# Engine programs in the main body instead of a block with a closing all-engine barrier

## The chip, the core and the metric

The kernel runs on one core of a Trainium2 chip. A core has five engines with an instruction stream each: TensorE (PE), VectorE (DVE), ScalarE (ACT), GpSimd (POOL) and SyncE (SP), which here issues 97 of the 98 transfers in the trace of before. In this kernel they meet only through semaphores (counters that one engine raises and another waits for). The time is in device microseconds (us), one number for each execution. Every execution also has a **span**: from the first to the last instruction that the profile records. Time and span are not the same, and this study is about the difference; I call it the **rest** (time less span of the same execution). Spans are listed to 0.1 us, so a single rest is good to about 0.05 us, plus the scatter between runs.

## The reference

One layer on 2048 tokens of width 640, in bfloat16: a layer norm, then a linear attention with 32 heads and a gated MLP side by side, and a residual.

```
xn  = layernorm(x)
out = x + linear_attention(xn; wqkv, w_phi, wo) + (silu(xn @ w1) * (xn @ w3)) @ w2
```

Its mathematics plays no part in what follows.

## The kernel before

The kernel records all operations in a list and orders them with a greedy scheduler of its own. It then makes one list per engine from them, of waits and operations with their semaphore updates. At the end of SyncE's list stand waits for all 17 output stores:

```python
    def emit(self, finish):
        ...
        for o in self.ops:
            ...                      # waits that o still needs, then o and what it signals
        for o in finish:             # the 17 output stores
            lists["SP"].append(("wait", o.sem[2], o.sem[1]))
        return lists
```

The lists are played into the five bodies of a block. Leaving the block emits an all-engine barrier:

```python
    lists = P.emit(finish)

    def play(items, eng):
        for it in items:
            if it[0] == "wait":
                eng.wait_ge(it[1], it[2])
            else:
                r = it[1]()
                if it[2] is not None:
                    r.then_inc(it[2], it[3])

    with nc.allow_low_precision(...), nc.allow_non_contiguous_dma(...), nc.Block() as block:

        @block.sync
        def _(e):
            play(lists["SP"], nc.sync)

        @block.tensor
        def _(e):
            play(lists["PE"], nc.tensor)
        ...                          # scalar, vector, gpsimd alike
```

A second all-engine barrier, at the entry, comes with the creation of the program object and stays (GpSimd's gathering starts at 0.600 us and the last engine is released by 0.783 us).

The softmax here doesn't subtract the row's maximum and nothing guards it: scores larger than these inputs give would overflow.

## Time and profile before

| | before |
|---|---|
| time, median of the first three runs | 267.78 us (267.52 to 267.91) |
| profiled execution: time, span, rest | 267.64, 265.86, 1.78 us |
| TensorE busy | 262.1 us, 99% of the span |
| last matmul done | 263.56 us |
| issue of the last output store | 263.92 us |
| end of the span | 265.86 us |

The page begins with the span and the busy time of each engine (PEld is TensorE's weight load):

```profile
span 265.9 us, 4695 instructions
...
PE 262.1 (99%) x1891; PEld 155.9 (59%) x1891; DVE 183.9 (69%) x313; ACT 106.3 (40%) x226; POOL 95.9 (36%) x107
...
PE 96%; DVE 1%; DMA 1%; POOL 0%; issue 0%
```

The last of these lines is the page's chain of work that ended last. The same chain in order of time (start, length, what) ends so:

```profile
7.07 0.05 issue
7.11 256.46 PE PS L104 x1867
263.57 0.02 issue
263.60 0.29 DVE xres L104
```

TensorE runs without a gap that the chain would name from 7.11 us to 263.57 us. So nothing in the middle can be won by changing how programs begin and end. The chain stops at VectorE's 0.29 us and doesn't tell of the 2 us behind it. What SyncE waits for from 264 us to the end does (waits in that window: us in total, times, longest):

```profile
SPq L929 <- DMA out_dram<-xres: 0.7, 2, 0.4
SPq L116 <- DVE xres L104: 0.2, 1, 0.2
SPq L935 <- PEq L935: 0.2, 1, 0.2
```

L929 is the waits on the output stores. L935 is the block: the closing barrier, where SyncE waits for its release. (The view names TensorE's sequencer; by the records below it is GpSimd that releases.) The views count semaphores, drains and jumps as no work, so here are the sequencers' records of the tail, taken from the trace (start in us, length in ns):

```
217.648  2669  POOL  drain                    (block)
225.259   629  ACT   drain, signals           (block)
262.251  1355  PE    drain, signals           (block)
263.611   330  DVE   drain, signals           (block)
263.917   332  SP    issue of the last store, 128x128
264.300    28  SP    wait for two stores; six of these follow, to 265.142
265.403    28  SP    wait for the last store and an older one
265.471    41  SP    jump, carrying the wait for one more old store
265.648     7  SP    drain, signals           (block)
265.681    17  POOL  has all four signals
265.759    17  POOL  releases the others
265.801    17  SP    released; ACT 265.805, DVE 265.812, PE 265.813 (51 ns: end of span)
```

### The profile page before, as it was taken

The numbers are of one execution on the slowest core, as the hardware profiler recorded it, in microseconds if no ns is written. First come the engines' busy times: TensorE is split into PE (matmuls) and PEld (weight loads), VectorE is DVE, ScalarE is ACT, GpSimd is POOL, SyncE is SP. The second block draws the span as 40 slices with busy tenths as digits, with TensorE's granted clock in tenths as the row PEclk, the third lists the DMA queues.
The fourth block names the chain that finished last, engine by engine and source line by source line (L and its number), as shares of the span: only waits on it lengthen the run. The fifth ranks groups of instructions, "written<-read, shape, count | busy, mean of one in ns | idle before, by whom it ended". The sixth has DMA issues, their size and how long they took to land.

```text
span 265.9 us, 4695 instructions
## 1 busy us (share of the span) xinstructions
PE 262.1 (99%) x1891; PEld 155.9 (59%) x1891; DVE 183.9 (69%) x313; ACT 106.3 (40%) x226; POOL 95.9 (36%) x107
## 2 busy tenths in 40 slices
PE   7999999999999999999999999999999999999996
PEld 3655545565558556465565756455656564777773
DVE  4668999999796679696685858788769567512112
ACT  5546988699760452251405240263143322000000
POOL 4221587989997035106030523007303321000000
DMA  6997088723301981932525070613260626141211
GB/s 211 270 307 205 8 161 242 162 52 55 117 2 22 270 195 39 140 56 62 94 49 128 2 159 25 131 25 75 62 133 22 132 52 128 27 123 52 87 39 49
DMA packets 62742, 27.73 MB, mean 104 GB/s; under 512 B 49920, under 2 KB 62720, under 8 KB 62720
## 3 DMA queue, kind: packets, MB, share of 16 engines
q1 hardware_dynamic: 62576, 27.26, 44.0%
q8 instruction: 15, 0.25, 0.4%
q10 hardware_dynamic: 144, 0.16, 0.2%
q14 instruction: 7, 0.06, 0.1%
HBM read 12.81 MB, written 2.62 MB: 58 GB/s over the span
## 4 chain that ended last, share of the span: by engine, by line
PE 96%; DVE 1%; DMA 1%; POOL 0%; issue 0%
PE PS L104 96%; DMA x_tok<-in_A_x_dram 1%; DVE bst L104 1%; DVE x_tok L104 0%; DVE mv L104 0%; POOL rstd L104 0%; DVE xres L104 0%
## 5 line engine op out<-in xcount | busy, mean ns | idle before, releaser
L104 PE MATMUL PS<-xnT,w_s 128*128 128x512 bf16 x480 | 108.2, 379 | 0.0
L104 PEld LDWEIGHTS PS<-xnT,w_s 128*128 128x128 bf16 x480 | 46.4, 98 | 50.9
L104 POOL TENSOR_TENSOR eqt<-eqt,rS 128x600 bf16<-128x600 bf16 (+1 forms) x32 | 41.0, 1306 | 97.4 <-DVE rS L104 97.4
L104 ACT ACTIVATE th<-PS 128x512 f32<-128x512 f32 x48 | 28.6, 596 | 79.0 <-PE PS L104 78.9
L104 PE MATMUL PS<-w_s,hT 128*128 128x320 bf16 (+2 forms) x384 | 54.9, 299 | 0.0
L104 DVE SCALAR_TENSOR_TENSOR t<-th,PS 128x512 bf16<-128x512 f32 x48 | 32.4, 675 | 31.4 <-ACT th L104 31.4
L104 PEld LDWEIGHTS PS<-w_s,hT 128*128 128x128 bf16 x384 | 37.1, 98 | 15.1
L104 PE MATMUL PS<-WVK,xnT 128*128 128x512 bf16 (+3 forms) x260 | 45.6, 330 | 0.1
L104 POOL TENSOR_TENSOR ekt<-ekt,rS 128x640 bf16<-128x640 bf16 x32 | 39.8, 1276 | 4.8 <-DVE rS L104 4.8
L104 ACT ACTIVATE eqt<-PS 128x240 bf16<-128x240 f32 (+1 forms) x96 | 27.2, 348 | 25.9 <-PE PS L104 24.1
L104 DVE TENSOR_TENSOR xres<-PS,xres 128x640 bf16<-128x640 f32 (+2 forms) x17 | 13.3, 782 | 33.5 <-PE PS L104 33.5
L104 PEld LDWEIGHTS PS<-WVK,xnT 128*128 128x128 bf16 x260 | 24.2, 98 | 19.4 <-ACT WVK L104 0.4
L104 DVE SCALAR_TENSOR_TENSOR hT<-t,PS 128x512 bf16<-128x512 bf16 x48 | 33.0, 687 | 1.7
L104 DVE TENSOR_REDUCE S<-ekt 128x64 f32<-128x1280 bf16 x16 | 23.3, 1455 | 2.2 <-ACT ekt L104 2.1
L104 PE MATMUL PS<-wo_s,oT 128*128 128x320 bf16 (+2 forms) x160 | 24.5, 299 | 0.0
L104 PE MATMUL PS<-Wqp,xnT 128*128 128x360 bf16 (+1 forms) x160 | 24.3, 299 | 0.0
L104 DVE TENSOR_REDUCE S<-eqt 128x66 f32<-128x1320 bf16 x16 | 24.2, 1510 | 0.0
L104 ACT ACTIVATE ekt<-PS 128x640 bf16<-128x640 f32 x32 | 22.3, 703 | 1.3 <-PE PS L104 0.8
L104 PEld LDWEIGHTS PS<-Wqp,xnT 128*128 128x128 bf16 x160 | 15.2, 98 | 7.6
L104 DVE RECIPROCAL rS<-S 128x64 f32<-128x64 f32 (+1 forms) x32 | 17.9, 560 | 1.1
L104 PEld LDWEIGHTS PS<-wo_s,oT 128*128 128x128 bf16 x160 | 15.2, 98 | 5.9
L104 DVE TENSOR_TENSOR o_tok<-PS,g_s 128x360 bf16<-128x360 f32 (+1 forms) x32 | 15.7, 491 | 1.1
(50 smaller groups left out, 124.3 us busy)
## 6 DMA issues: line engine op xcount, KB each, us to landing
w_s<-in_B_w_dram SPq DMA_DIRECT2D x6, 640.0 KB, 6.4
xres<-in_A_x_dram SPq DMA_DIRECT2D x16, 160.0 KB, 2.5
out_dram<-xres SPq DMA_DIRECT2D x15, 160.0 KB, 1.9
x_tok<-in_A_x_dram SPq DMA_DIRECT2D x3, 640.0 KB, 4.8
w_s<-in_B_w_dram SPq DMA_DIRECT2D x1, 1920.0 KB, 9.3
wo_s<-in_A_wo_dram SPq DMA_DIRECT2D x1, 800.0 KB, 4.8
WVK<-in_A_wqkv_dram SPq DMA_DIRECT2D x2, 320.0 KB, 4.5
x_tok<-in_A_x_dram SPq DMA_DIRECT2D x3, 160.0 KB, 2.7
```

The costliest lines, as they stand in the source:

```text
L104: o = _Op(eng, lambda: m(*args, **kw), r, w, cost)
```

## The change

The intent: no block, so no jumps and no barrier at the end. The waits on the output stores stay on SyncE. The outcome must be the same, since every dependence has its own semaphore.

```diff
-    with nc.allow_low_precision(...), nc.allow_non_contiguous_dma(...), nc.Block() as block:
-
-        @block.sync
-        def _(e):
-            play(lists["SP"], nc.sync)
-        ...                          # tensor, scalar, vector, gpsimd alike
+    with nc.allow_low_precision(...), nc.allow_non_contiguous_dma(...):
+        for e in ("SP", "PE", "ACT", "DVE", "POOL"):
+            play(lists[e], P.eng[e])
```

More of the change, by code (lines that the diff above doesn't have):

```diff
@@ L933, in play @@
                     r.then_inc(it[2], it[3])
-    with nc.allow_low_precision(reason="bf16 results"), nc.allow_non_contiguous_dma(reason="w_phi rows"), nc.Block() as block:
-        @block.sync
-        def _(e):
-            play(lists["SP"], nc.sync)
-        @block.tensor
-        def _(e):
-            play(lists["PE"], nc.tensor)
-        @block.scalar
-        def _(e):
-            play(lists["ACT"], nc.scalar)
-        @block.vector
-        def _(e):
-            play(lists["DVE"], nc.vector)
-        @block.gpsimd
-        def _(e):
-            play(lists["POOL"], nc.gpsimd)
+    with nc.allow_low_precision(reason="bf16 results"), nc.allow_non_contiguous_dma(reason="w_phi rows"):
+        for e in ("SP", "PE", "ACT", "DVE", "POOL"):
+            play(lists[e], P.eng[e])
 _INS = ['A_x', 'A_wqkv', 'A_w_phi', 'A_wo', 'B_x', 'B_w1', 'B_w3', 'B_w2']
```

## The prediction

> What bounds the kernel now. The span is 265.9 us; three timed runs gave a median of 267.78 us. The page shows TensorE busy 262.1 us (99%); the chain in order of time has one unbroken TensorE piece of 256.46 us, from 7.11 to 263.57 us. Before it stand 7 us of loading and normalising; after it 0.29 us of VectorE work, the last output store and the end of the program. The granted clock is 1.000.

> What the change does. The order of instructions shows every engine with the same work in the same order; only the jump at each end of each engine's program is gone. No wait between engines, no tile and no transfer changes. In the built program the jump into a block falls through: no branch record stands there in the trace, and behind the entry barrier, which stays, the first work follows as usual (VectorE after 0.13 us; elsewhere it needs 0.10 us from a semaphore wait to its next work). So the entry can gain 0.00 to 0.03 us.

> What is really removed is the closing barrier. By the sequencers' records in the trace, SyncE's last paired wait for output stores ends at 265.43 us; then come a branch that carries one more wait (265.47 us), SyncE's drain (265.65 us), the gathering on GpSimd's queue (265.68 us), its release (265.76 us) and the receipt on the four others (265.80 to 265.86 us). In the changed program SyncE ends on one more semaphore wait in the branch's place, as long as its others (0.03 us), so at about 265.50 us: 0.36 us off the end of the span. The drains of the four other engines end by 263.94 us and cost nothing now. The waits on the output stores stay, so the 1.5 us from the last store's issue (263.92 us) to the end of its wait stay too.

> All of this 0.36 us is on the critical path. With the entry the span should be about 265.5 us.

> Is it in the time too? The time is 1.9 us longer than the span. [...] I take the whole, plus a few hundredths.

> Prediction: 267.37 us, 0.15% less; 8 times in 10 between 266.9 and 267.8 us, a range made mostly of the spread of single runs (267.52 to 267.91) and of the unknown end of the program. Chances: faster by over 2% 0.01, within 2% 0.98, slower by over 2% 0.01.

> What would show the steps right: the span falls by 0.3 to 0.45 us; no drain stands at the end of any engine; SyncE's last record is a semaphore wait; the unbroken TensorE piece stays at 256.5 us within 0.3 us and begins within 0.1 us of 7.11 us. Wrong: a TensorE piece changed by over 0.5 us[...], or a span shorter by 0.36 us with an unchanged time (then the end outside the span takes the gain back).

> What would make the prediction wrong: the end outside the span costs more or less when engines arrive apart[...].

The sum of the forecast: 0.36 us for the tail, and 0.05 us for the entry (0.00 to 0.03 us) and the "few hundredths" together, make the 0.41 us from 267.78 to 267.37 us.

## More of the kernel before

The length of a drain's record is not a cost: GpSimd's runs from 217.648 to 220.317 us, but GpSimd's last piece of work ends at 220.250 us. The record contains that work.

## The result, and the profile after

| | before | after |
|---|---|---|
| time, median of 6 runs | 267.68 us (267.52 to 268.33) | 266.79 us (266.62 to 267.09) |
| ratio after to before, 95% interval | | 0.9964 [0.9951, 0.9977] |
| profiled execution: time, span, rest | 267.64, 265.86, 1.78 us | 266.92, 265.67, 1.25 us |
| tail: last store's issue to the end of the span | 1.947 us | 1.512 us |
| rest, all fast runs | 1.69 to 1.80 us (25 runs in the jobs below) | 1.19 to 1.26 us (6 runs) |

The ratio is the mean time of one kernel's fast runs over that of the other's of the same rounds, so it is not quite the ratio of the medians quoted here. The change is a gain of 0.4%, clear of noise but small. It is over twice the 0.41 us that I had forecast. It lies below the stated range. All outputs are right.

The page after, for the same lines:

```profile
span 265.7 us, 4684 instructions
...
PE 261.9 (99%) x1891; PEld 155.8 (59%) x1891; DVE 183.9 (69%) x313; ACT 106.2 (40%) x226; POOL 95.9 (36%) x107
...
PE 97%; DMA 1%; DVE 1%; ACT 0%; POOL 0%; issue 0%
```

The chain in order of time after:

```profile
6.66 0.10 issue
6.76 257.06 PE PS L104 x1871
263.81 0.02 issue
263.83 0.29 DVE xres L104
```

Two things mislead here. The span of this one execution fell by only 0.2 us (the six executions of after had spans of 265.4 to 265.9 us), and the TensorE piece looks 0.60 us longer. The piece counts 1871 matmuls in place of 1867: the chain now enters TensorE four matmuls earlier. Measured between the same two matmuls (the 25th and the last to start), TensorE took 256.23 us before and 256.28 us after. Of the 0.24 us by which the last matmul came later, 0.18 us are there at the 25th matmul already (7.30 us in place of 7.11 us). They were collected in the first 7 us, while the first loads land, and they are scatter between executions: three later programs with the same bodies started that matmul at 7.10 or 7.11 us (e5 with TensorE held, e8, e6), others at up to 7.67 us (e9), and e7's disturbed execution at 8.28 us.

Behind the last store the change is plain. SyncE's waits from 264 us on, after; the line of the barrier is gone:

```profile
SPq L929 <- DMA out_dram<-xres: 0.6, 2, 0.4
SPq L116 <- DVE xres L104: 0.2, 1, 0.2
```

And the records of the tail after:

```
264.154   332  SP    issue of the last store
264.538    17  SP    wait for one old store; seven waits for two stores follow
265.638    28  SP    wait for the last store and an older one (end of span)
```

No drain stands at the end of any engine. The records of the entry, up to the first load's issue at 0.805 us and VectorE's first work at 0.883 us, start at the same nanosecond as before, but for one drain of ScalarE that starts 5 ns earlier.

So the time fell by 0.89 us by the medians, or by 0.96 us by the ratio (0.0036 of 267.7 us). The tail gives 1.947 - 1.512 = 0.435 us of it, and the rest gives 1.75 - 1.23 = 0.52 us, in which no record of an instruction lies. Together they make 0.955 us.

### The profile page after: what moved, and what is told of

It reads as the page before. It is cut to its first block, busy times and chain, and to the rows that moved or that the text cites. A ratio compares the mean times of both kernels' runs of the same rounds, so it can differ in the third digit from the quotient of the medians.

```text
span 265.7 us, 4684 instructions
## 1 busy us (share of the span) xinstructions
PE 261.9 (99%) x1891; PEld 155.8 (59%) x1891; DVE 183.9 (69%) x313; ACT 106.2 (40%) x226; POOL 95.9 (36%) x107
## 4 chain that ended last, share of the span: by engine, by line
PE 97%; DMA 1%; DVE 1%; ACT 0%; POOL 0%; issue 0%
PE PS L104 97%; DMA x_tok<-in_A_x_dram 1%; DVE bst L104 0%; ACT xnT L104 0%; POOL rstd L104 0%; DVE x_tok L104 0%; DVE xres L104 0%; DVE mv L104 0%
```

## The experiments

The question that was left open by the views: why do 0.52 us vanish *outside* the span?

- **Theory A**: it is being held back. Behind its last record each engine has an end of the program that no view shows. Without the barrier four engines walk through theirs while SyncE still waits for the stores.
- **Theory B**: the jumps and separate bodies cost it, outside the span, at the entry or the end.
- **Theory C**: the drains cost it; they leave the engines in a state that takes longer to end.

All edits are to the kernel after, unless said. `play` is as above, and `finish[-2:]` are the stores of the last tile's two parts. All figures are of fast runs. The rests are medians of 4 to 6 runs each; those of before, run on the same chip in the same job, had medians of 1.75, 1.73 and 1.74 us in the three jobs. The kernel after itself was not run again in these jobs; its figures are those above.

### e1: the barrier without the block

```diff
         for e in ("SP", "PE", "ACT", "DVE", "POOL"):
             play(lists[e], P.eng[e])
+        nc.all_engine_barrier()
```

> The straight bodies with an all-engine barrier put back behind them: the barrier without the block and its jumps. 'Rest' is a run's time less its own span: 1.78 us in the profiled run of before, 1.22 us after. Theory A (it is the closing barrier: without it the four other engines go ahead into an end of the program that the span doesn't show): all of the gain goes, time as before (267.7 us, ratio 0.999 to 1.001), rest 1.7 to 1.85 us, and the span's tail from the last store's issue to the end again 1.95 us. Theory B (jumps and separate bodies cost the time, at the entry or at the end, outside the span): the rest stays near 1.22 us and only the 0.43 us of the tail come back, time about 267.2 us.

Measured: 267.50 us, ratio to before 0.9995 [0.9972, 1.0018]; rest 1.71 us. Theory B falls: with the straight bodies and no jump, the barrier alone brings the whole rest back. The tail was 1.757 us, not the 1.95 us that I expected. Before's tail thus has two parts: the barrier's (1.757 - 1.512 = 0.245 us) and 0.19 us of the jump that carried a wait.

SyncE's waits from 264 us on, in this kernel (L938 is the barrier):

```profile
SPq L116 <- DVE xres L104: 3.4, 2, 3.2
SPq L929 <- DMA out_dram<-xres: 0.6, 2, 0.4
SPq L938 <- PEq L938: 0.2, 1, 0.2
```

The barrier's line is back with the 0.2 us that it had before. (The 3.4 us of L116 are no change: the issue of the last store but one ends just behind 264 us here, so that its wait of 3.2 us falls into the window.)

### e2: drains, no barrier

```diff
             play(lists[e], P.eng[e])
+        for e in ("SP", "PE", "ACT", "DVE", "POOL"):
+            P.eng[e].drain()
```

> The straight bodies, each closed by a drain of its engine, without any semaphore between engines. Theory A (engines held back to a common end): drains don't hold the early engines, so rest stays about 1.22 us, and the time at most 0.1 us above after (SyncE's own drain). Theory C (the drains themselves cost, GpSimd's above all, in what follows): rest 1.5 to 1.8 us.

Measured: 267.00 us, ratio 0.9971 [0.9947, 0.9995]; rest 1.23 us. Theory C falls. The trace has the same drains as before (GpSimd 2669 ns, TensorE 1355 ns, VectorE 330 ns), only nobody waits for them. (As said, most of each length is the engine's own last work.)

### e3: a barrier without drains

```diff
             play(lists[e], P.eng[e])
+        nc.all_engine_barrier(sem_only=True)
```

> The straight bodies with a barrier made of semaphores alone, no drains. Theory A: rest 1.7 to 1.85 us as with the full barrier, span tail 0.2 to 0.4 us longer than after, time 267.4 to 267.8 us. Theory C (the drains cost): rest about 1.22 us, and only the tail grows.

Measured: 267.51 us by its four fast runs, ratio 0.9994 [0.9969, 1.0018]; rest 1.75 us. Its profiled execution (345.39 us at a granted clock of 0.756, the only one of the 59 executions of changed programs) isn't used for anything. The drains don't matter from this side either.

### e4: all engines wait, without a barrier

```diff
             play(lists[e], P.eng[e])
+        for e in ("PE", "ACT", "DVE", "POOL"):
+            for o in finish[-2:]:
+                P.eng[e].wait_ge(o.sem[2], o.sem[1])
```

> No barrier and no drain: the four other engines themselves wait, as SyncE does, for the landing of the last two output stores, and so end together with SyncE. Theory A: the span stays as after (within 0.1 us in its tail) and the rest rises to 1.7 to 1.85 us, time about 267.3 us: that would show that being held is what costs, not the barrier's own instructions. Theories B and C: rest about 1.22 us and time as after, 266.8 us.

Measured: 267.56 us, ratio 0.9991 [0.9968, 1.0014]; rest 1.76 us, with a tail of 1.542 us. This is the cleanest of the four. There is no gathering, no release, no drain and no jump. In the records all five engines see the last store land between 265.731 and 265.743 us. Yet half a microsecond more passes behind the span. SyncE's waits look as in the kernel after:

```profile
SPq L116 <- DVE xres L104: 3.4, 2, 3.2
SPq L929 <- DMA out_dram<-xres: 0.6, 2, 0.4
```

A reader of these two lines alone would say that nothing had changed (L116 as in e1). Being held is what costs, not the barrier's own instructions.

### e5: one engine held at a time

```diff
             play(lists[e], P.eng[e])
+        for o in finish[-2:]:
+            P.eng["PE"].wait_ge(o.sem[2], o.sem[1])      # or "ACT", "DVE", "POOL"
```

> Only TensorE waits for the last two stores beside SyncE; the other three go ahead. What is asked: is it one engine whose own end outside the span is long (rest 1.75 us for that engine, 1.23 us for the others), or does each held engine add a part (rests between 1.23 and 1.75 us, the sum of the four extras about 0.52 us)? My guess is that the steps behind the kernel pass from engine to engine, so that each held one adds a part: 1.3 to 1.5 us here.

> Only ScalarE waits beside SyncE. One long engine: rest 1.23 or 1.75 us. Parts: 1.3 to 1.5 us.

> Only VectorE waits beside SyncE. One long engine: rest 1.23 or 1.75 us. Parts: 1.3 to 1.5 us.

> Only GpSimd waits beside SyncE. One long engine: rest 1.23 or 1.75 us; were it one engine, GpSimd would be my guess, as its drain is the longest in the trace of before[...]. Parts: 1.3 to 1.5 us.

(GpSimd's drain in the trace of before: a record of 2.67 us, 0.067 us of it behind GpSimd's last work.)

| held beside SyncE | time, median | rest | over SyncE alone |
|---|---|---|---|
| none (after) | 266.79 us | 1.23 us | |
| VectorE | 266.93 us | 1.35 us | 0.12 us |
| ScalarE | 266.91 us | 1.40 us | 0.17 us |
| TensorE | 267.10 us | 1.50 us | 0.27 us |
| GpSimd | 267.42 us | 1.81 us | 0.58 us |

Single rests within a row lie within 0.1 us. Two of the sixteen executions took 269 us (one with TensorE, one with VectorE held); their spans were 2 us longer and their rests the same, so the rest is the sharper measure here. My guess of added parts fails: the four extras sum to 1.14 us, and all engines held together cost 0.53 us. GpSimd alone costs as much as all. That suggests a maximum: each engine has an end of its own length, and the time ends with the last of them. The other pure picture, one long engine and nothing for the rest, fails too, since the three others differ from 1.23 us.

The profile of the kernel with GpSimd held, by its span and its last pieces of work (timeline: start, length, engine, line, what):

```profile
core 0: 265.6 us, clock 1.000
...
263.54 0.88 SPq L116 DMA_DIRECT2D out_dram<-xres  x2
263.77 0.29 DVE L104 TENSOR_TENSOR xres<-PS,xres 128x128 bf16<-128x128 f32 x1 [0.26 <-PE PS L104]
```

And of the kernel after:

```profile
core 0: 265.7 us, clock 1.000
...
263.61 0.88 SPq L116 DMA_DIRECT2D out_dram<-xres  x2
263.83 0.29 DVE L104 TENSOR_TENSOR xres<-PS,xres 128x128 bf16<-128x128 f32 x1 [0.26 <-PE PS L104]
```

By the profile the first of these two executions is the faster one, by 0.05 us. By the measured time it is the slower one, by 0.49 us (267.41 against 266.92 us).

### e7: three held, GpSimd free

```diff
-        for e in ("PE", "ACT", "DVE", "POOL"):
+        for e in ("PE", "ACT", "DVE"):
             for o in finish[-2:]:                          # against e4
                 P.eng[e].wait_ge(o.sem[2], o.sem[1])
```

> TensorE, ScalarE and VectorE wait for the last two stores beside SyncE; GpSimd alone goes ahead. Held alone they gave rests of 1.50, 1.40 and 1.35 us over 1.23 us for SyncE alone. If every engine walks through an end of its own length and the longest sets the time (maximum): 1.50 us. If each held engine adds its part (sum): 1.23 + 0.27 + 0.17 + 0.12 = 1.79 us.

Measured: rest 1.52 us (1.48 to 1.55). The maximum said 1.50 us, the sum 1.79 us: the maximum holds. The times are no use here. Two of four runs were near 269 us, the profiled one (269.22 us) with a clock of 0.994 and its last matmul done at 265.81 us in place of 263.8 us; the rest was the same in all four.

### e8: GpSimd released one store earlier

```diff
             play(lists[e], P.eng[e])
+        o = finish[-2]
+        P.eng["POOL"].wait_ge(o.sem[2], o.sem[1])
```

> GpSimd waits for the last store but one only, which lands 0.29 to 0.30 us before the last; SyncE waits for both. Maximum: GpSimd's end of 1.81 us then starts 0.29 us before the end of the span, so rest 1.51 us (1.45 to 1.58). If it mattered only whether GpSimd waits at all or is the last to come: 1.8 us or 1.23 us.

Measured: rest 1.50 us (1.45 to 1.57), time 266.90 us. In the records GpSimd is released at 265.136 us, 0.288 us before the end of the span at 265.424 us, and 1.81 - 0.29 = 1.52 us. A late GpSimd costs to the extent that it is late, not for waiting as such.

### e6: the final waits on GpSimd alone

```diff
         for o in finish:
-            lists["SP"].append(("wait", o.sem[2], o.sem[1]))
+            lists["POOL"].append(("wait", o.sem[2], o.sem[1]))
```

> All final waits moved from SyncE to GpSimd, so GpSimd alone ends last and SyncE goes ahead. Maximum: rest 1.75 to 1.85 us, as with both held, time 267.3 to 267.5 us, though the program has no barrier and as few instructions as after. If the rest came from two or more engines meeting late: 1.23 us.

Measured: 267.28 us, ratio 0.9980 [0.9958, 1.0003]; rest 1.79 us. SyncE's last record ended at 264.39 us, 1.2 us before the end of the span, and it helped nothing. One engine, the last one and with a long end, is enough. So the kernel after is fast for two reasons at once: nothing holds the others, and the one engine that must wait for the stores is the one with the shortest end.

### e9: the jump without its wait (an edit to the kernel before)

```diff
         @block.sync
         def _(e):
             play(lists["SP"], nc.sync)
+            nc.sync.drain()
```

> The kernel before, with block and barrier, but a drain closes SyncE's body, so that the odd last wait hangs on it and not on the jump: the built program then has no branch that is taken. In the trace of before 0.14 us lie between the branch's end and the drain behind it. Expected: no branch record, tail from the last store's issue 1.95 us down to 1.76 to 1.82 us, rest unchanged at 1.75 us, time 0.13 to 0.19 us below before (the spread of single runs may hide it). If the block itself, not the waits on its jump, costs: tail still 1.95 us.

Measured: no jump is left in the trace; tail 1.823 us in place of 1.947 us; rest 1.73 us. The time (267.60 us, ratio 0.9997 [0.9975, 1.0019]) can't resolve 0.12 us and is inconclusive by itself. By the records, the added drain (266.145 us) takes the wait, and the barrier's drain starts 0.055 us after it; before, 0.177 us passed from the start of the jump to that drain. The block's barrier is unchanged, with the same line in SyncE's waits from 264 us on:

```profile
SPq L929 <- DMA out_dram<-xres: 0.7, 2, 0.4
SPq L935 <- PEq L935: 0.2, 1, 0.2
```

So the block's jumps on which nothing hangs left no record and cost nothing that could be measured (the entry records of before and after start within 5 ns of each other; the rest is 1.71 us in e1, without jumps, and 1.73 to 1.75 us in before), and the one with a wait cost 0.12 us (this run) to 0.19 us (e1, where the odd wait moved to the front of the row as well).

### What the maximum explains

Take for each engine the end that it showed when held: SyncE 1.23, VectorE 1.35, ScalarE 1.40, TensorE 1.50 and GpSimd 1.81 us from its last record to the end of the time. With the full barrier GpSimd gets past first: in the trace of before its last record ends at 265.776 us, 0.088 us before the end of the span. That gives 1.81 - 0.09 = 1.72 us, and 1.73 to 1.75 us were measured. In the kernel after GpSimd ends at 220.5 us, ScalarE at 226.1 us, TensorE at 263.8 us and VectorE at 264.1 us; by themselves they would let the time end by 265.5 us, long before SyncE's 265.67 + 1.23 = 266.9 us.

```
last to end        1      2      3      4      5      6      7      8      9 |  last | rest
SyncE (after) -1.693 -1.658 -1.620 -1.389  0.109  0.152  0.191  0.225  0.272 | 1.422 | 1.25
VectorE (e5)  -1.721 -1.687 -1.649  0.146  0.170  0.267  0.306  0.340  0.387 | 1.530 | 1.34
ScalarE (e5)  -1.712  0.114  0.153  0.197  0.220  0.318  0.357  0.391  0.438 | 1.584 | 1.39
TensorE (e5)   0.192  0.226  0.264  0.307  0.331  0.428  0.467  0.502  0.548 | 1.689 | 1.50
GpSimd (e5)   -1.709 -1.675  0.543  0.588  0.611  0.708  0.748  0.782  0.828 | 1.976 | 1.79
all (before)   0.239  0.273  0.484  0.529  0.552  0.649  0.688  0.724  0.770 | 1.957 | 1.78
```

Whichever engine is held, the row stops in front of one place: the first with TensorE, the second with ScalarE, the third with GpSimd, the fourth with VectorE, the fifth with SyncE. So in these six traces the engines do not end side by side. They are passed in this one order, and four steps follow. The maximum comes out of it: in each trace with one engine last, the ninth update came behind that engine's own and the steps after it, from 0.16 us later with SyncE to 0.36 us with TensorE. Behind the ninth update everything takes the same, whoever was last: 1.14 to 1.15 us to the last update in the traces of the fast runs, 1.19 us in that of before. The time, counted from the start of the span, ends 0.17 to 0.20 us ahead of the last update in all of them. The difference between the kernels is therefore the lateness of the ninth update: 0.27 us behind the span with SyncE last, 0.83 us with GpSimd. In the kernel after, four of the nine steps are done while SyncE still waits for the stores; in the kernel before, the barrier puts all nine behind the span.

GpSimd is not slow because of its place: behind its update the row needs 0.29 us to the ninth, behind TensorE's 0.36 us. But from GpSimd's last record to its update 0.53 to 0.54 us pass in e4, e5, e6 and e8 (0.57 us in before), and 0.11 to 0.19 us with the four others when held alone.

## Why the prediction was wrong

Point by point:

- **What bounds the kernel**: right. TensorE's stretch between the same matmuls is 256.23 and 256.28 us. The sign of failure that I named, a piece changed by over 0.5 us, did appear (256.46 to 257.06 us) and was a false alarm, since the chain counted four more matmuls. It should have been stated between two fixed instructions.
- **The entry gains 0.00 to 0.03 us**: right, and at its lower end: 0.00 us.
- **The tail**: "0.36 us off the end of the span". The mechanism was right and the size was off: 0.435 us. I let SyncE run one more wait behind its last one. In the changed program the odd wait came first in the row and was hidden under the landing of the last store (264.154 us issued, 265.666 us waited for: 1.512 us, as before's 1.514 us).
- **"I take the whole, plus a few hundredths"**: this is the term that failed. The reason for it was an assumption that no trace had shown. I gave what happens outside the span a few hundredths of a microsecond where the runs show 0.52 us, more than the tail itself. I had read the 1.9 us between span and time as a constant. In fact it depends on which engine comes last, from 1.23 us (SyncE) to 1.81 us (GpSimd). What ending early is worth: in the trace of after, four of the nine updates of semaphore 2 lie over a microsecond before the end of the span, while in that of before the barrier delays all nine to behind it (0.239 to 0.770 us).
- **The range**: made of the spread of single runs and a small allowance for the end of the program. The allowance was the one number that no view could supply, and so deserved the width. The list of semaphore updates in the trace of before did hold it: the row starts only when the barrier has let go of TensorE, and takes 0.53 us.

What stays open: the updates behind the span are recorded, the instructions that make them are not. So no run shows why GpSimd needs 0.54 us to its update, nor what fills the 1.14 us behind the ninth beyond the updates themselves. Taking away the entry barrier as well was not tried; it comes with the program object. No version beat the kernel after.

## What to carry to other kernels

In a kernel on one core, don't end with an all-engine barrier when every output already has its own wait: here it cost 0.25 us inside the span, up to 0.19 us for a jump with a wait on it, and 0.52 us that no line of the profile's views shows. Let one engine wait for the last stores, and let it be SyncE, not GpSimd (rest 1.23 us in the kernel after, 1.79 us in e6); an engine that isn't needed for the last few microseconds should be free to finish. And compare times, not spans, when a change touches the end of a program: the kernel with GpSimd held had the shorter span and the longer time.
